# Block 0 of a fused attention and gated feed-forward kernel, laid out with two tokens per row

## Chip, cores, metric

One core of one Trainium2 chip. The metric is the device time in microseconds (us) of one execution. The profile's span of an execution is some 1.8 us shorter than its time; both are used here, and it is said which.

## The reference

Linear attention with a decay per head, then a feed-forward layer with a sigmoid gate. The sizes are B = 4 batches, H = 8 heads, S = 768 tokens, D = 64, d_model = 512 and d_ff = 1536.

```python
def _attn_ref(q, k, v, lam):            # cut: shapes and casts
    for b in range(nb):                 # blocks along the sequence
        intra = einsum('bhic,bhjc->bhij', qb, kb) * Dmask     # lam**(i-j) for i >= j, else 0
        intra = einsum('bhij,bhjd->bhid', intra, vb)
        inter = einsum('bhid,bhde->bhie', qb * lam_pow, kv_state)
        out[block] = intra + inter
        kv_state = lam_block * kv_state + einsum('bhsd,bhse->bhde', kb * rev_pow, vb)

def _moe_ref(x, w_gate, w_val, w_out):
    gate = 1.0 / (1.0 + np.exp(-(x @ w_gate)))
    return gate * (x @ w_val) @ w_out
```

The kernel takes blocks of C = 128 tokens, six in all, which gives the same result. It works in bf16 with sums in 32 bits.

## The kernel before

Block 0 has to be loaded, transposed, scored, masked and multiplied before the first gate product can start; from then on the six blocks are interleaved so that TensorE (PE) always has work. Loads go out from Pool's queue, stores and the transposing copies of later blocks from SP's queue. Cuts are marked.

```python
    osb = ctx.enter_context(tc.tile_pool(name="osb", bufs=4))       # output buffers "ob"
    # ... other pools; PSUM: ps_at 5 banks, ps_ff 3 banks

    def load(n, what, b0, b1):
        # ... (blocks 2 and later: even and odd heads apart)
            nc.gpsimd.dma_start(                # one token per partition, pieces of 64 values
                out=lst[n][:, b0:b1],
                in_=src[b0:b1, :, sl, :].rearrange("b h s d -> s (b h) d"))

    # constants: iotas, identity and triangle on Pool; masks "mask" (DVE) and decay table "lamq" (ACT)
    # are built before the first block is worked on

    def idle(n):                                # filler: keeps PE's clock up while loads are under way
        for i in range(n):
            nc.tensor.matmul(wm, lhsT=zero[:, :128], rhs=zero, start=True, stop=True, ...)

    def c(n, *pairs):                           # state products: 32 for all of block 0
        # ...
                        nc.tensor.matmul(cp[half(u), i, hp, :], lhsT=kdh(n, 2 * bp + i, h),
                                         rhs=V[n][:, 2 * bp + i, h, :], ...)

    def piece_po(n, tt):
        # ... output product of 128 tokens
        ob = osb.tile([128, DM], FP32, tag="ob", name="ob")
        nc.scalar.copy(ob, po)
        nc.sync.dma_start(out=out[tt * S + n * C:tt * S + (n + 1) * C, :], in_=ob)

    load_gv(0, GW)
    idle(10)
    piece_tq0([0, 1])                           # transposes of q, scaled by lamq on DVE
    idle(4)
    piece_tk0(0)                                # transposes of k, copied by ACT
    idle(2)
    piece_s(0, [0])                             # scores
    piece_m(0, 0)                               # masked on DVE (one half of two batches on Pool)
    # ... the other three batches, load_gv(1), load_gv(2), fillers
    piece_a0(0); piece_a0(1); idle(2); piece_a0(2); piece_a0(3, True); idle(2)   # intra products

    make_kd(0)                                  # Pool
    load_gv(3, GW)
    # ... further loads
    gv(0, 0, 1, 2, 3, 4)                        # gate and value products, five of twelve
    c(0, 0, 1)
    # ...
```

Of the kernel before, what the change touches and what calls it, by code (L numbers as in the profile page):

```python
# [16 lines left out]
def kernel(  # L17
# [78 lines left out]

    nc.scalar.preload_act_table_set("natural_log_exp_and_others")
    ident = const.tile([128, 128], BF16, tag="ident")
    zero = const.tile([128, TCH], BF16, tag="zero")
    jn = const.tile([128, 2], FP32, tag="jn")  # L100
    ip1 = const.tile([128, C], FP32, tag="ip1")
    tri = const.tile([128, C], FP32, tag="tri")
    nc.vector.memset(zero, 0.0)  # L103
    nc.vector.memset(ident, 0.0)
    nc.vector.memset(tri, 0.0)
    Sb = stp.tile([128, B, HP, D], BF16, tag="Sb", name="Sb")
    nc.vector.memset(Sb, 0.0)

    load(0, "q", 0, 2)
    load(0, "k", 0, 2)  # L110
    for i, base in enumerate((-1, C - 1)):
        nc.gpsimd.iota(jn[:, i:i + 1], pattern=[[0, 1]], base=base, channel_multiplier=-1,
                       allow_small_or_imprecise_dtypes=True)
    make_identity(nc, ident, nomemset=True)
    nc.gpsimd.iota(ip1, pattern=[[1, C]], base=1, channel_multiplier=0,
                   allow_small_or_imprecise_dtypes=True)
    nc.gpsimd.affine_select(out=tri, in_=tri, compare_op=ALU.is_gt, fill=1.0, base=0,
                            pattern=[[-1, C]], channel_multiplier=1)
    load(0, "k", 2, 4)
    load(0, "q", 2, 3)  # L120
    load(0, "q", 3, 4)
    load(0, "v", 0, 2)
    load(0, "v", 2, 3)
    load(0, "v", 3, 4)

    lnl = const.tile([128, H], FP32, tag="lnl")
    nc.scalar.activation(lnl, lam_bc, AF.Ln)
    pk = const.tile([128, H], FP32, tag="pk")
    nc.scalar.activation(pk, lnl, AF.Exp, scale=jn[:, 0:1])
    lnp = const.tile([128, HP], FP32, tag="lnp")  # L130
    for u in range(2):
        us = slice(u * 64, (u + 1) * 64)
        nc.scalar.activation(lnp[us, :].rearrange("p (e x) -> p e x", e=2),
                             lam_bc[us, :].rearrange("p (x u e) -> p u e x", u=2, e=2)[:, u], AF.Ln)
    lamq = const.tile([128, HP, C], BF16, tag="lamq")
    for hp in range(HP):
        nc.scalar.activation(lamq[:, hp, :], ip1, AF.Exp, scale=lnp[:, hp:hp + 1])
    kds = const.tile([128, H], FP32, tag="kds")
    nc.scalar.activation(kds, lnl, AF.Exp, scale=jn[:, 1:2])
    dec = const.tile([128, HP], FP32, tag="dec")  # L140
    nc.scalar.activation(dec, lnp, AF.Exp, scale=float(C))
    nc.scalar.preload_act_table_set("sigmoid_and_others")
    mask = const.tile([128, 2, HP, C], FP32, tag="mask")
    for u in range(2):
        nc.vector.tensor_tensor(
            out=mask[:, u].rearrange("p (e x) c -> p e x c", e=2),
            in0=tri.unsqueeze(1).unsqueeze(1).to_broadcast([128, 2, 2, C]),
            in1=pk.rearrange("p (x u e) -> p u e x", u=2, e=2)[:, u].unsqueeze(3).to_broadcast([128, 2, 2, C]),
            op=ALU.mult)
# [6 lines left out]

    def transpose(out, x, b, g):
        for u in range(2):
            nc.tensor.transpose(out[half(u)], x[:, b, head(g, u), :], ident)  # L159

    wm = ps_ff.tile([128, TCH], FP32, name="wm", tag="ff")

    def idle(n):
        for i in range(n):
            nc.tensor.matmul(wm, lhsT=zero[:, :128], rhs=zero, start=True, stop=True,  # L165
                             skip_group_check=True)
# [22 lines left out]
    def piece_tq0(bs):  # L189
        tq = ps_at.tile([128, 2, 2, 2 * C], BF16, name="tq", tag="ps")  # L190
        for b in bs:
            if (0, b // 2) not in QS:
                QS[0, b // 2] = trsb.tile([128, 2, 2, 2, C], BF16, tag="QS", name="QS")
            for g in range(HP):
                transpose(tq[:, b % 2, g // 2, g % 2 * C:g % 2 * C + C], Q[0], b, g)
        for b in bs:
            nc.vector.tensor_tensor(out=QS[0, b // 2][:, :, b % 2].rearrange("p e x c -> p e (x c)"),
                                    in0=tq[:, b % 2], in1=lamq_e, op=ALU.mult)

    def piece_tk0(bp):  # L200
        tk = ps_at.tile([128, 2, 2, 2 * C], BF16, name="tk", tag="ps")
        for i in range(2):
            for g in range(HP):
                transpose(tk[:, i, g // 2, g % 2 * C:g % 2 * C + C], K[0], 2 * bp + i, g)
        KS[0, bp] = trsb.tile([128, 2, 2, 2, C], BF16, tag="KS", name="KS")
        for i in range(2):
            nc.scalar.copy(KS[0, bp][:, :, i].rearrange("p e x c -> p e (x c)"), tk[:, i])
# [32 lines left out]
    def piece_m2(n, b, part):  # L240
        if part:
            nc.vector.tensor_tensor(out=MT[n, b][:, 0], in0=SP[n, b][0], in1=mask[:, 0], op=ALU.mult)
            return
        MT[n, b] = mtp.tile([128, 2, HP, C], BF16, tag="MT", name="MT")
        sc = const.tile([128, HP, C], FP32, tag="sc", bufs=2)
        nc.scalar.copy(sc, SP[n, b][1])
        nc.gpsimd.tensor_tensor(out=MT[n, b][:, 1], in0=sc, in1=mask[:, 1], op=ALU.mult)

# [4 lines left out]

    def intra(n, b, out, m, start, stop):
        for e in range(2):
            nc.tensor.matmul(out[half(e)], lhsT=V[n][:, b, 2 * m + e, :],  # L256
                             rhs=MT[n, b][:, m % 2, 2 * e + m // 2, :],
                             start=start, stop=stop, skip_group_check=True)

    def piece_a(n, pairs):  # L260
# [12 lines left out]
        for bp in pairs:  # L273
            for u in range(2):
                for i in range(2):
                    for x in range(2):
                        intra(n, 2 * bp + i, OP[bp, u][:, x, i, :], 2 * x + u, False, i == 1 and x == 1)
# [6 lines left out]
    def piece_a0(b, split=False):  # L284
        if 0 not in XT:
            XT[0] = xtp.tile([128, NMT, B, C], BF16, tag="XT", name="XT")
        w = 2 if split else NMT
        for m0 in range(0, NMT, w):
            op = ps_at.tile([128, w, C], FP32, name="op", tag="ps")
            for m in range(w):  # L290
                intra(0, b, op[:, m, :], m0 + m, m == 0, m == w - 1)
            if split and m0 == 0:
                nc.vector.tensor_copy(XT[0][:, m0:m0 + w, b, :], op)
            else:
                nc.scalar.copy(XT[0][:, m0:m0 + w, b, :], op)
# [28 lines left out]
    def c(n, *pairs):  # L324
        for bp in pairs:
            pool, tag = (ps_at, "ps") if bp == 0 else (ps_ff, "ff")
            cp = pool.tile([128, 2, HP, D], FP32, name="cp", tag=tag)
            for i in range(2):
                for hp in range(HP):
                    for u in range(2):  # L330
                        h = head(hp, u)
                        nc.tensor.matmul(cp[half(u), i, hp, :], lhsT=kdh(n, 2 * bp + i, h),  # L332
                                         rhs=V[n][:, 2 * bp + i, h, :], start=(i == 0 and hp == 0),
                                         stop=(i == 1 and hp == HP - 1), skip_group_check=True)
            dst = Sb[:, 2 * bp:2 * bp + 2]
            if n == 0:
                nc.vector.tensor_copy(dst, cp)
            else:
                nc.vector.tensor_tensor(out=dst, in0=cp, in1=SD.pop(bp), op=ALU.add)  # L339
# [50 lines left out]
    def piece_po(n, tt):  # L390
# [6 lines left out]
        nc.sync.dma_start(out=out[tt * S + n * C:tt * S + (n + 1) * C, :], in_=ob)  # L397
# [5 lines left out]
    idle(10)  # L403
    piece_tq0([0, 1])
    idle(4)
    piece_tk0(0)
    idle(2)
    piece_s(0, [0])
    piece_m(0, 0)
    piece_s(0, [1])  # L410
    piece_m2(0, 1, 0)
    piece_tk0(1)
    piece_tq0([2])
    piece_m2(0, 1, 1)
    load_gv(1, GW)
    idle(3)
    piece_tq0([3])
    piece_s(0, [2], ps_ff, "ff")
    piece_m2(0, 2, 0)
    piece_m2(0, 2, 1)  # L420
    load_gv(2, GW)
    piece_s(0, [3])
    piece_m(0, 3)
    idle(3)
    piece_a0(0)
    piece_a0(1)
    idle(2)
    piece_a0(2)
    piece_a0(3, True)
    idle(2)  # L430

    make_kd(0)
    load_gv(3, GW)
    load(1, "qk", 0, 2)
    load_gv(4, GW)
# [7 lines left out]
    def t(n, bp):  # L443
        piece_t(n, bp)
# [19 lines left out]
    gv(0, 0, 1, 2, 3, 4)  # L464
    c(0, 0, 1)
    fade()
    make_kd(1)
    gv(0, 5, 6, 7)
# [7 lines left out]
    gv(0, 11)  # L476
    t(1, 1)
    load(2, "qkv", 0, B)
    transpose_by_dma(2)
    gvh(1, 0, 0, 1)  # L480
# [89 lines left out]
```

## Time and profile before

| | us |
|---|---|
| time, median of 3 runs | 230.43 (230.3 to 230.69) |
| span of the profiled execution, which was not one of the three and took 231.89 | 230.1 |
| first gate product starts | 19.17 |
| block 0's first output product starts | 67.92 |
| block 3's first gate product starts | 126.75 |

The first view is the chain of waits on the page: the work that ended last, followed back to the start, as shares of the span by engine and then by line.

```profile
PE 92%; DMA 3%; POOL 2%; issue 1%; DVE 0%; POOLq 0%
PE po L393 26%; PE gp L348 25%; PE vp L354 24%; DMA qb<-in_q_dram 3%; PE sp L235 3%; PE gp L365 3%; PE op L256 3%; PE vp L371 3%; PE op L268 1%; PE wm L165 1%; PE cp L332 1%; PE po L382 1%; POOL kb L84 1%; PE tq L159 1%; PE tk L159 0%
```

PE is the limit. Anything that is not PE work is at the start, which the same chain gives piece by piece (start, length, what):

```profile
5.80 6.72 DMA qb<-in_q_dram
...
16.05 0.94 PE wm L165 x3
19.34 0.86 PE gp L348 x4
20.20 0.86 PE vp L354 x4
```

The windows view gives the busy time of each engine in stretches of the span; PEclk is the clock granted to PE, 1.00 being full.

```profile
core 0: us, PE busy (x) PEld busy (x) DVE busy (x) ACT busy (x) POOL busy (x), PEclk, DMA share, GB/s
12.00:16.00 4.00, 3.37 (x45) 1.80 (x41) 1.96 (x4) 1.55 (x3) 2.69 (x3) 0.62 2.04 172
20.00:25.00 5.00, 5.00 (x24) 2.25 (x23) 1.75 (x3) 1.79 (x3) 5.00 (x5) 1.00 0.97 124
25.00:30.00 5.00, 4.95 (x52) 2.46 (x52) 2.89 (x5) 1.59 (x3) 5.00 (x7) 1.00 1.78 157
85.00:100.00 15.00, 14.80 (x155) 7.73 (x156) 4.02 (x6) 6.20 (x11) 9.74 (x8) 1.00 0.50 115
```

From 20 us on PE is busy almost without a gap.

From the view of the output tensor, the time from issue to landing, and from the timeline of SP's queue the first block's stores and the two transposing copies that block 3 needs (start, length):

```profile
DMA to landing us min/median/max: 1.7/2.0/6.1
```

### The profile page before, as it was taken

Reading aid. Unit: us, or ns where it says so; the run is one execution under the profiler, and the core shown is the slowest. Engines: PE = TensorE matmul, PEld = TensorE weight load, DVE = VectorE, ACT = ScalarE, POOL = GpSimd, SP = SyncE. Lnnn points to the kernel's source line nnn. Section 1 sums busy time; section 2 is a strip of 40 time slices with the busy share of each in tenths; the row PEclk is TensorE's granted clock in tenths of the full one; section 3 lists DMA queues with packets and bytes.
Section 4 is the critical chain, followed back from the end, with each engine's and each line's share of the span. In section 5 each row is a group of like instructions: output and inputs, shape, how many; then the busy total and the mean of one; then the engine's idle time right before and its main releaser. Section 6 shows DMA issues by size and latency. Waiting matters only on the chain.

```text
span 230.1 us, 4267 instructions
## 1 busy us (share of the span) xinstructions
PE 220.9 (96%) x1766; PEld 112.1 (49%) x1790; DVE 95.3 (41%) x157; ACT 80.5 (35%) x147; POOL 81.9 (36%) x78
## 2 busy tenths in 40 slices
PE   7689999999999999999999999999999999999994
PEld 2344444688544446444446444446444445444442
DVE  3352456485341352244752244662244750333300
ACT  5525334544332224434224433224433224433221
POOL 8979998693980003970002970000000000000000
PEclk9979999999999999999999999999999999999999
DMA  8999999999999922799912799912740012100022
GB/s 52 144 177 174 122 181 170 182 198 158 152 158 153 218 108 91 159 145 144 57 48 94 153 139 147 68 46 94 151 78 0 3 46 94 46 0 0 3 91 91
DMA packets 102595, 24.92 MB, mean 108 GB/s; under 512 B 91696, under 2 KB 99632, under 8 KB 102576
## 3 DMA queue, kind: packets, MB, share of 16 engines
q0 software_dynamic: 82192, 14.16, 95.2%
q1 hardware_dynamic: 20384, 10.49, 19.1%
q8 instruction: 14, 0.23, 0.4%
q14 instruction: 5, 0.04, 0.1%
HBM read 28.32 MB, written 6.29 MB: 150 GB/s over the span
## 4 chain that ended last, share of the span: by engine, by line
PE 92%; DMA 3%; POOL 2%; issue 1%; DVE 0%; POOLq 0%
PE po L393 26%; PE gp L348 25%; PE vp L354 24%; DMA qb<-in_q_dram 3%; PE sp L235 3%; PE gp L365 3%; PE op L256 3%; PE vp L371 3%; PE op L268 1%; PE wm L165 1%; PE cp L332 1%; PE po L382 1%; POOL kb L84 1%; PE tq L159 1%; PE tk L159 0%
## 5 line engine op out<-in xcount | busy, mean ns | idle before, releaser
L357 DVE TENSOR_TENSOR ht<-sg,vp 128x512 bf16<-128x512 bf16 x65 | 44.7, 688 | 78.6 <-PE vp L354 74.4
L348 PE MATMUL gp<-XT,WG 128*128 128x512 bf16 x252 | 66.2, 379 | 0.7 <-issue 0.2
L354 PE MATMUL vp<-XT,WV 128*128 128x512 bf16 x256 | 65.9, 379 | 0.0
L351 ACT ACTIVATE sg<-gp 128x512 bf16<-128x512 f32 x65 | 38.8, 597 | 70.8 <-PE gp L348 70.6
L393 PE MATMUL po<-WO,ht 128*128 128x512 bf16 x266 | 61.3, 379 | 0.5
L393 PEld LDWEIGHTS <-ht 128*128 128x128 bf16 x276 | 26.2, 98 | 31.2
L354 PEld LDWEIGHTS <-WV 128*128 128x128 bf16 x260 | 25.4, 98 | 30.7
L348 PEld LDWEIGHTS <-WG 128*128 128x128 bf16 x260 | 24.8, 98 | 29.5 <-issue 0.3
L252 DVE TENSOR_TENSOR MT<-sp,mask 128x512 bf16<-128x512 f32 x44 | 27.8, 683 | 14.4 <-PE sp L235 14.4
L396 ACT COPY ob<-po 128x512 f32<-128x512 f32 x23 | 13.5, 585 | 52.5 <-PE po L393 45.8
L317 POOL TENSOR_TENSOR sd<-Sb,dec 128x512 f32<-128x512 bf16 x8 | 8.1, 1035 | 44.9 <-DVE Sb L339 44.8
L308 POOL TENSOR_TENSOR kd<-kb,kds 128x1024 bf16<-128x1024 bf16 x6 | 11.3, 1905 | 4.0 <-DMA kb<-in_k_dram 4.0
L84 POOL DMA_DIRECT2D vb<-in_v_dram x9 | 12.2, 1367 | 0.0
L339 DVE TENSOR_TENSOR Sb<-cp,sd 128x512 bf16<-128x512 f32 x8 | 5.2, 686 | 15.5 <-PE cp L332 15.5
L282 ACT CAST XT<-op 128x512 bf16<-128x512 f32 x20 | 10.4, 598 | 3.0 <-PE op L256 3.0
L165 PE MATMUL wm<-zero 128*128 128x512 bf16 x24 | 9.1, 515 | 1.7 <-DVE zero L103 1.2
L78 POOL DMA_DIRECT2D qb<-in_q_dram x8 | 9.5, 1185 | 0.0
L78 POOL DMA_DIRECT2D kb<-in_k_dram x8 | 9.2, 1171 | 0.0
L365 PE MATMUL gp<-XT,WG 128*128 128x256 bf16 x56 | 8.4, 273 | 0.0
L371 PE MATMUL vp<-XT,WV 128*128 128x256 bf16 x56 | 8.4, 272 | 0.0
L302 POOL TENSOR_TENSOR kd<-kb,kds 128x1024 bf16<-128x1024 bf16 x4 | 7.6, 1912 | 2.1 <-DMA kb<-in_k_dram 2.1
L375 DVE TENSOR_TENSOR ht<-sg,vp 128x256 bf16<-128x256 bf16 x14 | 5.8, 419 | 5.1 <-PE vp L371 4.1
(59 smaller groups left out, 124.9 us busy)
## 6 DMA issues: line engine op xcount, KB each, us to landing
out_dram<-ob SPq DMA_DIRECT2D x23, 256.0 KB, 2.0
kb<-in_k_dram POOLq DMA_DIRECT2D x12, 256.0 KB, 9.9
qb<-in_q_dram POOLq DMA_DIRECT2D x11, 256.0 KB, 8.7
vb<-in_v_dram POOLq DMA_DIRECT2D x4, 512.0 KB, 13.3
WG<-in_moe_w_gate_dram POOLq DMA_DIRECT2D x6, 256.0 KB, 7.3
WV<-in_moe_w_val_dram POOLq DMA_DIRECT2D x6, 256.0 KB, 7.9
WO<-in_moe_w_out_dram POOLq DMA_DIRECT2D x3, 512.0 KB, 14.2
vb<-in_v_dram POOLq DMA_DIRECT2D x3, 256.0 KB, 10.5
```

The source lines that it names most:

```text
L78: nc.gpsimd.dma_start(out=lst[n][:, e].rearrange("p b y d -> p (b y) d"), in_=src[:, e::2, sl, :].rearrange("b y s d -> s (b y) d"))
L84: nc.gpsimd.dma_start(out=lst[n][:, b0:b1], in_=src[b0:b1, :, sl, :].rearrange("b h s d -> s (b h) d"))
L165: nc.tensor.matmul(wm, lhsT=zero[:, :128], rhs=zero, start=True, stop=True, skip_group_check=True)
L252: nc.vector.tensor_tensor(out=MT[n, b][:, u], in0=SP[n, b][u], in1=mask[:, u], op=ALU.mult)
L348: nc.tensor.matmul(gp, lhsT=WG[:, mt, fs], rhs=x[:, mt, :], start=(mt == 0), stop=(mt == NMT - 1))
L351: nc.scalar.activation(sg, gp, AF.Sigmoid)
L354: nc.tensor.matmul(vp, lhsT=WV[:, mt, fs], rhs=x[:, mt, :], start=(mt == 0), stop=(mt == NMT - 1))
L357: nc.vector.tensor_mul(HT[n, ft], sg, vp)
L365: nc.tensor.matmul(gp[:, cs], lhsT=WG[:, mt, fs], rhs=x[:, mt, cs], start=(mt == 0), stop=(mt == NMT - 1))
L371: nc.tensor.matmul(vp[:, cs], lhsT=WV[:, mt, fs], rhs=x[:, mt, cs], start=(mt == 0), stop=(mt == NMT - 1))
L393: nc.tensor.matmul(po, lhsT=HT[n, ft][:, tt * 128:(tt + 1) * 128], rhs=WO[:, ft, :], start=(ft == 0), stop=(ft == NFT - 1))
L396: nc.scalar.copy(ob, po)
```

## The change

The intent is to start the gate products sooner. Block 0's q, k and v are laid out with two neighbouring tokens in one row: a batch's 128 tokens take 64 partitions, two batches share a tile, and a piece of the load is 128 values long instead of 64. So there are half as many pieces, and one load per batch. The products of block 0 then run on quarters of the PE array (64 x 64), and its tokens come out in a permuted order (even tokens, then odd ones), which the store has to undo. Pool loses its iotas (DVE makes the constants), and the second weight slice is issued before Pool's one mask product. The tables that only blocks 1 and later need are made on DVE between the first gate products.

```diff
+    R = 2
+    SR = C // R
+    Q0, K0, V0 = (qkv.tile([128, NB2, H, R, D], BF16, tag=c + "b", name=c + "b") for c in "qkv")
+    def load0(t, src, b):
+        nc.gpsimd.dma_start(
+            out=t[b % 2 * 64:b % 2 * 64 + 64, b // 2].rearrange("p h r d -> p h (r d)"),
+            in_=src[b, :, 0:C, :].rearrange("h (s r) d -> s h (r d)", r=R))
+    # ... twelve loads: q0 k0 q1 k1 q2 q3 k2 k3 v0 v1 v2 v3; constants on DVE in place of Pool's iotas
+    def make_lamq():
+        nc.vector.tensor_copy(lamq.rearrange("p g (s r) -> p g r s", r=R),
+                              lam0.rearrange("p g (r s) -> p g r s", r=R))
+        nc.vector.tensor_scalar(out=tri, in0=ip1, scalar1=p1, scalar2=None, op0=ALU.is_ge)
+    def make_mask(u):
+        nc.vector.tensor_tensor(out=mask[:, u]..., in0=tri..., in1=pk..., op=ALU.mult)
+    # ... turn0, piece_s0, piece_a0: transposes, scores and intra products on 64 x 64 quarters
+    def piece_c0():                       # 64 state products instead of 32
         ob = osb.tile([128, DM], FP32, tag="ob", name="ob")
         nc.scalar.copy(ob, po)
-        nc.sync.dma_start(out=out[tt * S + n * C:tt * S + (n + 1) * C, :], in_=ob)
+        dst = out[tt * S + n * C:tt * S + (n + 1) * C, :]
+        nc.sync.dma_start(out=dst.rearrange("(s r) m -> r s m", r=R) if n == 0 else dst, in_=ob)
     GW = DFF // 6
     load_gv(0, GW)
-    idle(10)
-    piece_tq0([0, 1])
-    idle(4)
-    piece_tk0(0)
-    # ...
+    idle(6, True)
+    piece_tq0(0)
+    idle(1)
+    piece_tk0(0)
+    # ... scores of the second pair of batches:
+    piece_s0(1)
+    load_gv(1, GW)
+    piece_m0(1, 0, 0, True)               # Pool's mask product
+    # ... intra products of both pairs, fillers
     load_gv(2, GW)
     load_gv(3, GW)
     load(1, "qk", 0, 2)
+    make_kd0()                            # Pool's state product
-    gv(0, 0, 1, 2, 3, 4)
-    c(0, 0, 1)
+    gv(0, 0)
+    make_lamq()
+    gv(0, 1)
+    make_mask(0)
+    gv(0, 2)
+    make_mask(1)
+    gv(0, 3, 4, 5, 6)
+    piece_c0()
     # ... t(1, 1) half a gate product later
```

## The prediction

> **What bounds it now.** The chain of waits is 92% PE; from 19.2 us on PE is back to back (windows view: 9.95 of 10 us busy from 20 to 30, 14.79 of 15 from 30 to 45). All that can be won is the start: the first gate product begins at 19.17 us (timeline). Before it the chain reads: Pool issuing loads to 5.80, a q load landing at 12.5, then transposes, scores, masks, intra products and filler matmuls. Issue-to-landing times give landings of q01 6.3, k01 8.4, k23 11.5, q2 12.5, q3 13.4, v3 16.4, WG0 17.7, WV0 19.05, WG1 20.4, WV1 21.8. The granted clock is 0.59 and 0.72 from 12.5 to 17.5 us (windows).
>
> **What changes.**
> - Two tokens per row halve the descriptors of block 0. From q01 to v3, 1280 KB (as written) landed in 10.1 us, 127 KB/us; v3 to WV1, with pieces four times as long, 1024 KB in 5.4 us, 190 KB/us. A line through the two gives about 163 KB/us for the new pieces (estimate), so block 0's 1.5 MB takes 9.4 instead of 12 us. This fits the Trainium skill, "DMA: Bandwidth & Descriptors", section Specifications, which wants at least 512 B per piece for line rate. Pool spacing per issue is 1.14 us (2048 pieces), 0.86 (1024), 0.74 (512-piece weights); I take 0.74 for the twelve new loads. The iotas leave Pool (0.9 us).
> - Estimated landings: q0 4.7, k1 7.0 to 8.5, k3 10.1 to 11.7, v3 13.3 to 14.9, WG0 14.7, WV0 16.
> - Then the chain is on ACT and DVE: lam0 ready about 6.1, KS copies, seven small ACT tables (about 1.4 us) before the second KS copy, about 8.5; first pair's scores; four mask products (0.68 each) and two scalings (0.42) on DVE to about 12.4; second pair's masks to about 14.5; intra products, copies (0.42 each). Ideal gate start 15.7; such sums come out about 0.8 us early, so 16.6 us.
> - Pool's product (1.3 us) waits for the second weight slice's issues (ending about 13.1), about when its input is ready: little cost. In return slice 2 lands before it is needed (19.5 us).
> - Cost: block 0's state products become 64 quarter-array matmuls instead of 32. Before, 32 took 0.63 us; the existing 64x64 products take 22 ns each, so about 1.4 us: +0.8 us on PE's path. The Trainium skill, "TensorEngine Tiling (Array Packing)", section Instruction Overhead, warns not to take tiling from a dimension already small; 64 columns is that case. The extra mask tables fall on DVE, which has room (0.69 of each 1.73 us used).
>
> **Sum.** Gate start 19.2 to 16.6 saves 2.6; state products give back 0.8; 0.3 for slips: about 1.5 us. Everything after block 1 is unchanged PE work. Predicted 228.9 us, range 227.4 to 230.4. Chances: faster by over 2% 0.04, within 2% 0.93, slower by over 2% 0.03.
>
> **What would show it.** First gate matmul between 15.6 and 17.6 us; last block 0 k landing near 11 instead of 11.5-13.4; Pool issues of block 0 at about 0.74 us each; state products 1.2 to 1.6 us; the rest of the chain still PE, same stretches of the same length, no new DMA wait at the gate products.
>
> **What would make it wrong.** Loads into 64 partitions using fewer engines, so landing no sooner; self-dependent small DVE operations delaying ident and masks; the table load holding back the KS copies; a colder clock at the gate start (filler cut from ten to six at first) costing up to 1 us; weight slices becoming the limit (WV0 cannot be used before about 16 us), which caps the gain near 3 us; DVE products plus four state copies holding PSUM buffers and stalling PE.

## More of the kernel before

```profile
71.32 22.02 SPq L397 DMA_DIRECT2D out_dram<-ob  x8
93.45 2.00 SPq L176 DMA_TRANSPOSE QR<-qb  x1
95.55 2.89 SPq L176 DMA_TRANSPOSE KR<-kb  x1
```

The two copies are issued at 93 and 95 us, long before block 3's scores.

## The result

| | before | after |
|---|---|---|
| time, median of 4 runs, us | 230.37 (230.3 to 230.69) | 239.02 (238.37 to 239.62) |
| span of the profiled execution | 230.1 | 237.1 |
| first gate product starts | 19.17 | 18.58 |
| block 0's first output product starts | 67.92 | 69.66 |
| block 3's first gate product starts | 126.75 | 133.31 |

The ratio is 1.037, with a 95% interval of 1.034 to 1.040: slower. A ratio here is the mean time of one kernel's fast runs over the mean of the other's in the same rounds, so it is not quite the ratio of the medians. All runs counted were fast.

Differences of the rows give a budget of the 7.0 us between the two spans: -0.6 before the first gate product; +2.3 from there to the first output product (48.75 before, 51.08 after); +4.8 from there to block 3's gate products (58.83 before, 63.65 after); +0.4 for the rest. So there are two losses, both in stretches that the prediction took as unchanged, and hardly any gain at the start.

The medians differ by 8.65 us and the spans by 7.0, because the profiled execution of the kernel before, at 231.89 us, was slower than any of its timed runs, and slow at the start. Against the usual execution that b_look shows below (230.15 us, span 228.4, with the same marks at 17.13, 66.19 and 125.02) the budget is 8.7 us: +1.5 before the first gate product, then +2.0, +4.8 and +0.4. By that look the start is a third loss.

### Second stretch: 20 to 30 us

The windows view of the changed kernel:

```profile
core 0: us, PE busy (x) PEld busy (x) DVE busy (x) ACT busy (x) POOL busy (x), PEclk, DMA share, GB/s
20.00:25.00 5.00, 3.92 (x19) 1.67 (x17) 4.42 (x4) 1.44 (x3) 5.00 (x5) 1.00 1.28 160
25.00:30.00 5.00, 4.17 (x19) 1.85 (x19) 4.14 (x6) 1.19 (x2) 5.00 (x6) 1.00 2.10 166
85.00:100.00 15.00, 12.04 (x141) 6.13 (x140) 3.02 (x6) 4.21 (x8) 8.00 (x6) 1.00 0.28 99
```

PE has lost 1.9 us between 20 and 30 us, and DVE is now busy 8.6 of 10 us. The timeline of the same stretch (start, length, engine, line, what; in brackets the idle time before it and what ended it):

```profile
21.18 1.75 DVE L200 COPY lamq<-lam 128x512 bf16<-128x512 bf16 x1
...
21.41 1.19 POOL L84 DMA_DIRECT2D kb<-in_k_dram  x1
...
22.57 3.95 POOL L393 TENSOR_TENSOR kd<-kb,kd 128x1024 bf16<-128x1024 bf16 x2
...
22.83 1.92 DVE L202 TENSOR_SCALAR tri<-ip,tok 128x128 f32<-128x128 f32 x1
...
25.26 1.81 DVE L205 TENSOR_TENSOR mask<-tri,pk 128x512 f32<-128x512 f32 x1
25.39 1.02 PE L458 MATMUL gp<-XT,WG 128*128 128x512 bf16 x4 [1.47 <-DVE ht L467]
...
27.59 0.68 DVE L205 TENSOR_TENSOR mask<-tri,pk 128x512 f32<-128x512 f32 x1
27.72 1.02 PE L458 MATMUL gp<-XT,WG 128*128 128x512 bf16 x4 [0.44 <-DVE ht L467]
```

The two masks are the same operation on the same shapes. The first, begun while Pool's state product (kd) is running, takes 1.81 us; the second, begun after it, takes 0.68. The small triangle, 128 values per partition, takes 1.92 us. While DVE is held up, the product ht of gate and value waits behind it, keeps its two PSUM banks, and PE stops: 1.47 and 0.44 us.

### Third stretch: 80 to 118 us

The chain of waits, shares of the span and then pieces in order of time:

```profile
PE 75%; DMA 14%; SPq 3%; DVE 3%; issue 1%; ACT 1%; POOL 1%; ACTq 0%; DVEq 0%; POOLq 0%
```

```profile
69.82 10.38 PE po L503 x48
80.22 0.59 ACT ob L506
80.83 17.49 DMA out_dram<-ob
98.43 0.59 ACT ob L506
99.59 6.59 SPq L240
106.28 11.48 DMA KR<-kb
117.81 0.62 PE sp L351 x16
```

An output store has taken a place in the chain. ACT waits for stores to land before it can reuse an output buffer, and what PE needs from ACT comes late (two stops of PE, 1.5 and 1.3 us, by the view of its waits); SP, which issues stores and transposing copies in one order, comes to block 3's copies at 99.59 instead of 93.45; the copies take longer to issue and to land; and block 3's scores wait for them (1.3 us). The view of ACT's waits (us in total, times, longest) has a line that the kernel before doesn't have:

```profile
ACT ob L506 <- DMA out_dram<-ob: 11.2, 3, 4.5
```

The view of the output tensor has a new maximum, and SP's queue is later and slower:

```profile
DMA to landing us min/median/max: 1.7/2.2/14.8
```

```profile
73.06 26.31 SPq L508 DMA_DIRECT2D out_dram<-ob  x8
99.59 6.59 SPq L240 DMA_TRANSPOSE QR<-qb  x1
106.28 5.76 SPq L240 DMA_TRANSPOSE KR<-kb  x1
```

The 14.8 us are those of block 1's first store, which SP issues behind block 0's four; for the four themselves the trace has no landing.

The edit says what is different about block 0's four stores. Before, a store writes 128 rows of 512 values, 128x512. After, block 0's write 2x64x512: the permutation has put a dimension of size 2 outermost. (In the trace's operands, `dst_num_elem=[128,1]` has become `[64,2]` for these four.) The packets in the trace show what that does. A store has 128 packets of 2 KB; the table gives the stretch from the first packet's start to the last one's end, and how many were under way at a time (the sum of their lengths over the stretch):

```
                                stretch us    under way    one packet, ns
before, a store in steady state      0.82         13            85
after, block 0, first store          5.45          2.1          89
after, block 0, second store         5.13          2.1          84
```

A packet takes as long as ever; there are two at a time instead of thirteen.

### The start

The new loads behaved much as predicted. Landings, from issue and time to landing: the last k at 11.65 us (estimated 10.1 to 11.7), the last v at 14.55 (13.3 to 14.9). Pool took 0.68 to 0.82 us for each of the new issues (0.74). But the first weight slices landed at 16.62 and 18.00 us, not at 14.7 and 16, and the gate began at 18.58, not 16.6. In the usual execution of the kernel before (b_look) the last v landed at 15.58 us and the slices at 16.73 and 18.07. So the new layout brought block 0's last v 1.0 us sooner, and the weights that the gate and value products also need only 0.1 us.

### The profile page after: what moved, and what is told of

The parts are those of the page before. It is cut to its first block, busy times and chain, and to the rows that moved or that the text cites. A ratio compares the mean times of both kernels' runs of the same rounds, so it can differ in the third digit from the quotient of the medians.

```text
span 237.1 us, 4639 instructions
## 1 busy us (share of the span) xinstructions
PE 223.9 (94%) x1946; PEld 113.4 (48%) x1946; DVE 105.6 (45%) x191; ACT 80.8 (34%) x152; POOL 80.0 (34%) x76
## 3 DMA queue, kind: packets, MB, share of 16 engines
q0 software_dynamic: 76112, 14.16, 82.0%
q1 hardware_dynamic: 20328, 10.49, 20.2%
## 4 chain that ended last, share of the span: by engine, by line
PE 75%; DMA 14%; SPq 3%; DVE 3%; issue 1%; ACT 1%; POOL 1%; ACTq 0%; DVEq 0%; POOLq 0%
PE po L503 21%; PE gp L458 19%; PE vp L464 19%; DMA out_dram<-ob 7%; DMA KR<-kb 5%; SPq L240 3%; PE gp L475 3%; PE vp L481 2%; DMA kb<-in_k_dram 2%; PE sp L351 2%; PE wm L229 2%; PE op L379 2%; PE po L492 1%; PE op L369 1%; PE tp L262 1%
## 5 line engine op out<-in xcount | busy, mean ns | idle before, releaser
L458 PE MATMUL gp<-XT,WG 128*128 128x512 bf16 x260 | 66.9, 379 | 4.9 <-DVE ht L467 1.9
L464 PE MATMUL vp<-XT,WV 128*128 128x512 bf16 x260 | 66.7, 379 | 0.0
L503 PEld LDWEIGHTS <-ht 128*128 128x128 bf16 x276 | 26.3, 98 | 31.2
L359 DVE TENSOR_TENSOR MT<-sp,mask 128x512 bf16<-128x512 f32 x40 | 25.2, 682 | 13.3 <-PE sp L351 13.3
L421 POOL TENSOR_TENSOR kd<-kb,kds 128x1024 bf16<-128x1024 bf16 x6 | 11.4, 1906 | 0.7 <-DMA kb<-in_k_dram 0.6
L84 POOL DMA_DIRECT2D vb<-in_v_dram x6 | 9.3, 1543 | 0.0
L478 ACT ACTIVATE sg<-gp 128x256 bf16<-128x256 f32 x14 | 5.4, 384 | 7.0 <-PE gp L475 7.0
## 6 DMA issues: line engine op xcount, KB each, us to landing
vb<-in_v_dram POOLq DMA_DIRECT2D x4, 512.0 KB, 14.2
WO<-in_moe_w_out_dram POOLq DMA_DIRECT2D x3, 512.0 KB, 13.3
```

Source lines behind the costliest of these rows:

```text
L359: nc.vector.tensor_tensor(out=MT[n, b][:, u], in0=SP[n, b][u], in1=mask[:, u], op=ALU.mult)
L421: nc.gpsimd.tensor_tensor(out=KD[n][:, e], in0=K[n][:, e], in1=kds[:, e::2].unsqueeze(1).unsqueeze(3).to_broadcast([128, B, HP, D]), op=AL ...
L458: nc.tensor.matmul(gp, lhsT=WG[:, mt, fs], rhs=x[:, mt, :], start=(mt == 0), stop=(mt == NMT - 1))
L464: nc.tensor.matmul(vp, lhsT=WV[:, mt, fs], rhs=x[:, mt, :], start=(mt == 0), stop=(mt == NMT - 1))
L503: nc.tensor.matmul(po, lhsT=HT[n, ft][:, tt * 128:(tt + 1) * 128], rhs=WO[:, ft, :], start=(ft == 0), stop=(ft == NFT - 1))
```

## The experiments

Theory S: the store's outermost dimension of 2 keeps it on few DMA engines; this is the third stretch's loss. Its rival is the row order itself: every second row of the output, an address pattern and not a shape. Theory P: DVE's tables wait for Pool; this is the second stretch's loss. Its rival D: DVE's new tables are slow, or too many, by themselves. Theory C: PE ran at half clock through much of the changed start. Its rival: the weight slices' landing sets the gate's start.

The kernel before was run again beside each set: 230.89 us (median of 7) beside the first four runs, 230.05 (one run) beside the three looks, 230.77 (11 runs) beside the two warmer kernels and the one with less filler, and 230.98 and 230.84 (7 each) beside the last two.

### a_store: block 0's store as two stores of 64 rows

The change, with the same rows going to the same addresses by other shapes:

```diff
-        nc.sync.dma_start(out=dst.rearrange("(s r) m -> r s m", r=R) if n == 0 else dst, in_=ob)
+        if n == 0:
+            for r in range(R):
+                nc.sync.dma_start(out=dst.rearrange("(s r) m -> r s m", r=R)[r],
+                                  in_=ob[r * SR:(r + 1) * SR])
+        else:
+            nc.sync.dma_start(out=dst, in_=ob)
```

> The changed kernel with block 0's store made as two stores of 64 rows each, one for each token of the pair; rows still go to every other row of the output. Theory S (a store whose outermost dimension is 2 is spread over few DMA engines, lands in 10 to 15 us and holds the output buffers, ScalarE and so TensorE): stores of block 0 land in 2 to 6 us as in the kernel before, no wait of ScalarE for an output store, about 4.8 us come back: 234.2 us. Rival (alternate rows in memory, or the loads of block 3 beside them, are what is slow): stores stay slow, 238 to 239 us.

Measured: 233.67 us (232.98 to 234.44), ratio to before 1.012 (1.008 to 1.015), correct. ACT no longer waits for a store; block 3's copies are issued at 94.98 and 97.35 us and take 2.27 and 2.82. The rows still go to every second row of the output, so the address pattern is not the cause; the shape is. This is 5.4 us of the loss (239.02 less 233.67; the two medians are from different sets of runs).

### a_tables: the tables four gate products later

```diff
-    gv(0, 0)
+    gv(0, 0, 1, 2, 3, 4)
     make_lamq()
-    gv(0, 1)
+    gv(0, 5)
     make_mask(0)
-    gv(0, 2)
+    gv(0, 6)
     make_mask(1)
-    gv(0, 3, 4, 5, 6)
```

> The changed kernel with the late tables (lamq copy, tri, two masks) on VectorE after gate products 4, 5 and 6 instead of 0, 1 and 2, so after Pool's state product of block 0 (which ended at 26.5 us). Theory P (VectorE operations with their inputs in SBUF wait while Pool's product runs): tri back from 1.92 to about 0.2 us, first mask from 1.81 to 0.68, no TensorE gap at the second and third gate products, about 2.1 us come back: 236.9 us. Rival (the tables are simply too much or too slow work for VectorE between the gate products): the same gap, later; 238.5 to 239.5 us.

Measured: 240.34 us (238.29 to 241.66), ratio 1.040 (1.033 to 1.046). The time was missed, the mechanism not: the tables now take 0.45, 0.99 and 0.68 us, no gate product waits for DVE, and from the first gate product to the first output product it takes 48.85 us, as in the kernel before. But in the profiled run the gate started at 20.84 us, so that the output products began at 69.69, where they began in the changed kernel (69.66); and the rest, with block 0's first store now spread over 7.0 us, was 2.4 us longer. The gain of this part could not be seen as time while the stores were there and the start wandered. It had to be measured with the stores mended.

### a_both: both edits

The two edits above together.

> Both repairs. If the two losses are separate and additive: 239.0 - 4.8 - 2.1 = 232.1 us. If they overlap (the delay at the tables hides part of the store delay): 233 to 235 us. If the start of the changed kernel is really worth 1.5 us as predicted: 229 us.

Measured: 232.06 us (231.88 to 233.08), ratio 1.006 (1.003 to 1.010), correct. Against a_store it is 1.6 us less, which is what the tables' place cost in time once the stores were mended (the ranges of the two just touch). The stretch from the first gate product to the first output product is 48.85 us (48.75 before). What is left, 1.2 us, lies ahead of the gate, which began at 19.50 us in this profile.

### b_store: the kernel before, with the new form of store alone

The result is wrong: rows that are not permuted are stored as if they were.

```diff
-        nc.sync.dma_start(out=out[tt * S + n * C:tt * S + (n + 1) * C, :], in_=ob)
+        dst = out[tt * S + n * C:tt * S + (n + 1) * C, :]
+        nc.sync.dma_start(out=dst.rearrange("(s r) m -> r s m", r=2) if n == 0 else dst, in_=ob)
```

> The kernel before with only the new store form of block 0 (alternate rows, outermost dimension 2); its rows come out in the wrong order on purpose. Theory S: stores land in 10 to 15 us, ScalarE waits for output stores, time 230.4 + 4.8 = 235.2 us. Rival (something else in the changed kernel slows that stage): 230 to 231 us.

Measured: 241.53 us (239.01 to 243.02; one of the four runs was slow), ratio of the fast ones 1.042 (1.035 to 1.049). The direction is that of theory S, the size twice what was expected. ACT's wait for stores, in its view of waits:

```profile
ACT ob L396 <- DMA out_dram<-ob: 20.2, 4, 6.1
```

The first two stores spread over 7.0 and 6.7 us, not 5.3, with 1.8 packets under way. Block 3's loads were under way beside them: the load of v for block 3, issued at 66.5 us, landed 31.2 us later (in the kernel before after 14.3 to 14.4). It is likely that the two slow each other on the engines that they share; the trace doesn't say which engine moves a packet. The longest stop of PE, 5.4 us, was for a copy of block 2's intra result that ACT could make only after standing 6.1 us in front of a store. So what such a store costs depends on what happens to be loading beside it; why this kernel fared worse than the changed one beyond that was not taken apart.

### b_law: four outermost sizes, where nothing else loads

The kernel before with block 4's four stores reshaped, to outermost sizes of 16, 8, 4 and 2. Its output is wrong, which doesn't matter for the time.

```diff
+        if n == 4:
+            dst = dst.rearrange("(s r) m -> r s m", r=16 >> tt)
```

> The kernel before, with the four stores of block 4 (a quiet stage for loads) written with outermost dimensions of 16, 8, 4 and 2 in this order (rows in wrong order on purpose). Theory S: time to landing grows as the outermost dimension shrinks, about 2, 2.5 to 3, 4 and 6 us or more; with 16 no slower than the plain form (2.0). Rival (alternate rows are what is slow): all four alike, 16 being the most scattered and no better than 2.

One look, 230.21 us beside 230.05. From the packets:

```
outermost size    stretch us    under way
128 (others)           0.82         13
16                     1.27         12.3
8                      2.44          7.1
4                      4.33          3.7
2                      6.26          2.1     (overlaps the one before it)
```

The number of packets under way follows the outermost size, up to 16, and each halving makes the stretch 1.4 to 1.9 times as long. The size of 16 was not quite as quick as the plain form (1.27 us against 0.82, landing after 2.93 us against 2.0, where no loss was expected); for the three smaller sizes the trace has no landing, so the stretches have to serve. This is what the Trainium skill says, in "DMA: Bandwidth & Descriptors", section "Why a DMA increments its semaphore by 16 and not by 1": the number of engines is the largest one up to 16 that divides the slowest dimension that isn't of size 1, on both sides of the transfer. The same page's "Rules for kernel authors" has it as a rule: "Put a dim whose size is a multiple of 16 (ideally the 128 partitions) outermost". The time did not move, and ACT's view of waits has no wait for a store: the cost of such a store is not its length but what queues behind it.

### a_nokd: the changed kernel without Pool's state product

Wrong: the state is computed from k without its decay.

```diff
-    make_kd0()
+    KD[0] = K0
```

> The changed kernel without Pool's state product of block 0 (the keys are used unscaled: wrong result on purpose), the tables left where they are. Theory P: tri takes about 0.2 us and both masks 0.68, no TensorE gap at gate products 2 and 3; about 2 us faster than the changed kernel, near 237 us. The lamq copy tells a side question: if it drops well below 1.75 us it too was waiting on Pool, if not it is slow in itself. Rival (tables too slow in themselves): durations as in the changed kernel, 239 us.

One look. The time, 240.38 us, was not the 237 expected; as in a_tables the gate began later (19.38 us) and the stretch of the stores took longer. But no gate product waits for DVE, and from the first gate product to the first output product it takes 48.84 us, as in the kernel before. DVE's timeline, with the tables at their place between the first gate products:

```profile
21.98 0.45 DVE L200 COPY lamq<-lam 128x512 bf16<-128x512 bf16 x1
22.32 0.89 DVE L202 TENSOR_SCALAR tri<-ip,tok 128x128 f32<-128x128 f32 x1
...
23.70 0.69 DVE L205 TENSOR_TENSOR mask<-tri,pk 128x512 f32<-128x512 f32 x1
```

At the same place and without Pool's product the triangle takes 0.89 us instead of 1.92 (not 0.2 as expected) and the first mask 0.69 instead of 1.81: theory P, and not D. The Trainium skill, "SBUF — State Buffer", section "Who interferes with whom", states it: a DVE instruction with two SBUF inputs contends with a Pool instruction that reads SBUF, copies and operations with a scalar may contend in a two-port mode, and whoever comes first holds the shared ports for its whole instruction. The mask has two SBUF inputs, the copy and the triangle one. The copy lamq (1.75 us in the changed kernel) began before Pool's product, beside Pool's issuing of loads, and was done 0.36 us after the product began. Here it took 0.45 us, and here too Pool was issuing a load beside it (of k, 21.87 to 23.18 us); in a_both it took 0.47 us beside an issue. So issuing alone did not hold it up there, and what did in the changed kernel stays open.

### b_look: the kernel before, once more

> The kernel before, unchanged, for a second look at its start. The first profile had a granted clock of 0.59 to 0.72 from 12.5 to 17.5 us. If that is peculiar to that execution, the first gate product comes about 1 to 1.5 us before 19.17 us here, and the changed start (18.58 us) gained nothing; if it belongs to the kernel, 19.2 us again.

One look, 230.15 us beside 230.05 for the kernel before. The line of the timeline to read is the first gate product:

```profile
17.13 1.02 PE L348 MATMUL gp<-XT,WG 128*128 128x512 bf16 x4
```

It starts at 17.13 us and not at 19.17, at full clock. In two further profiles of the kernel before with a change only later on, b_law and b_store, it starts at 17.53 and 17.87. The first profile, on which the prediction stands, was the late one.

### a_warm: both edits, and more filler

First fillers eight instead of six, six instead of two behind the first key transposes, one more at three places further on, one less at one.

```diff
-    idle(6, True)
+    idle(8, True)
     ...
-    idle(2)
+    idle(6)
     ...
+    idle(1)
     piece_tk0(1)
     ...
-    idle(2)
+    idle(3)
     piece_s0(0)
     ...
```

> Both repairs, and more filler matmuls on TensorE in the start (8 instead of 6 first, 6, 1 and 3 instead of 2, 0 and 2 in the waits for loads, one more before the last key transposes, one fewer before the last intra products). Theory C (the changed start loses because TensorE runs at half clock from about 6 to 13 us, its filler having been cut): fillers and transposes at full rate after about 8 us, first gate product near 17.2 us instead of 18.1 to 20.8, then bound by WV0's landing (18.0); time 230.0 to 230.9, against 232.1 for both repairs alone. Rival (the start is bound by the loads and the VectorE chain whatever the clock): first gate product at 18.5 us or later, 231.5 to 232.5 us.

Measured: 230.21 us (229.68 to 233.85, where one of six runs was slow), ratio 0.9965 (0.994 to 0.999), correct. That is 1.9 us less than a_both, from filler alone. The reason can be read from the fillers themselves in the timelines. The changed kernel, and then a_both:

```profile
9.31 1.04 PE L229 MATMUL wm<-zero 128*128 128x512 bf16 x2
...
14.19 0.60 PE L229 MATMUL wm<-zero 128*128 128x512 bf16 x2
```

```profile
14.37 0.61 PE L229 MATMUL wm<-zero 128*128 128x512 bf16 x1
```

In the changed kernel the same two fillers take 1.04 us at 9.3 us and 0.60 at 14.2: PE ran at about half rate until some 12 us. In a_both's profile, where the start is the same program, a single filler still takes 0.61 us at 14.4. In a_warm:

```profile
8.38 0.82 PE L229 MATMUL wm<-zero 128*128 128x512 bf16 x3
...
13.69 0.28 PE L318 MATMUL op<-MT,vb 64*64 64x128 bf16 x6
15.69 0.58 PE L318 MATMUL op<-MT,vb 64*64 64x128 bf16 x26 [1.73 <-issue]
```

Three fillers in 0.82 us: full rate already. The gate nevertheless began only at 18.02, not at 17.2 as expected, because of the last line: PE stood still for 1.73 us in the middle of 32 intra products and waited for no semaphore ("issue").

### a_split: the first weight slice in two halves

```diff
     GW = DFF // 6
-    load_gv(0, GW)
+    for lo in range(0, GW, 128):
+        nc.gpsimd.dma_start(out=WG[:, :, lo:lo + 128], in_=wg_r[:, :, lo:lo + 128])
+        nc.gpsimd.dma_start(out=WV[:, :, lo:lo + 128], in_=wv_r[:, :, lo:lo + 128])
```

> As a_warm, with the first weight slice loaded in two halves of 128 columns, so that the first gate and value products need half the bytes. If WV0's landing is the limit at the warm clock: first value product about 1 us sooner after the block's loads, 0.3 to 0.8 us faster than a_warm, 229.3 to 230.4 us. Rival (the limit is elsewhere, or the smaller pieces cost more than they free): same as a_warm or slower by up to 0.5 us.

Measured: 230.08 us (229.65 to 231.42, six runs), ratio 0.998 (0.995 to 1.000); gate at 17.75 us, the same stop of 1.57 us. As good as a_warm and no better: the first slices landed at 15.75 and 16.54 us, but with the stop there their landing was not what PE waited for. So a run that settles the rival to theory C, the slices' landing, is missing.

### b_idle6: the kernel before, with less filler

```diff
-    idle(10)
+    idle(6)
```

> The kernel before with its first filler matmuls cut from ten to six, as the change did, and nothing else. Theory C: the clock is not or less often released in the start, fillers of 0.43 us each after 6 us, first gate product 1 to 2 us later than its usual 17.1 to 17.9; 231 to 232.5 us. Rival: no difference, 230.2 to 230.9 us.

Measured: 230.67 us (230.36 to 231.2, six runs), ratio 0.999 (0.997 to 1.001): no difference. PE was at half rate until about 9 us in it, but at full rate by 9.6, and at 18.61 us its value products waited for the weights to land. For the kernel before, theory C missed: a cold start of that length is hidden behind the loads. That it cost the changed kernel time because there it lasted into the scores and the second pair's work is a reading of the two timelines and was not tested.

### a_fetch: what is the stop in a_warm?

The stop sits at the 448th PE instruction (weight loads and products counted) in a_warm and a_split, and also, with 0.39 and 0.18 us, in the changed kernel and a_store, although there other products stand at that place. So a number in the program, not an operand, seems to decide it. To shift the number, a_warm's first eight fillers of 512 columns become four each of 128 columns, 48 instructions more.

```diff
-    idle(8, True)
+    idle(8, True, True)          # each filler as four of 128 columns
```

> a_warm with its first eight filler matmuls of 512 columns each replaced by four of 128 columns: the same PE work, 48 more PE instructions ahead of everything else. In a_warm PE stood still for 1.73 us inside block 0's intra products at its 448th instruction, waiting for no semaphore; in three other kernels the stop fell on the same number at other operations. Theory I (PE's instructions for what follows have not arrived yet, their fetch queues behind the loads): the stop moves 48 instructions earlier in the program, into the second pair's score products, which break in two about 13.3 us and go on only at 15 to 15.7; the intra products then run with no such stop of their own. Rival W (the intra products wait for data, the last v load or a mask product): the score products run unbroken in about 0.85 us from 13.1, and the stop of 1.5 us or more stays inside the intra products. Time about 230 to 231 us under either.

Measured: 229.48 us (229.24 to 231.25, five runs), ratio 0.994 (0.991 to 0.998), correct. For its question it was inconclusive. The profiled run was the slowest of the five; PE was at half rate until 9.6 us in it, reached the second scores at 14.87 us only, and the timeline shows no stop. Both theories allow that, if what was missing had arrived by then. (From start to start, though, there is a trace of one: the 15th of the second scores, which is the 448th instruction here, begins 0.21 us after the 14th, at 15.44 us; in the changed kernel that step is 0.04 us.)

### a_fetch2: the same question with PE kept warm

a_warm, with one of its six fillers behind the first key transposes replaced by twelve of 64 columns: 22 instructions more.

```diff
-    idle(6)
+    idle(5)
+    for i in range(12):
+        nc.tensor.matmul(wm[0][:, :64], lhsT=zero[:, :128], rhs=zero[:, :64], start=True, stop=True, ...)
```

> The run before left PE at half clock until 9.6 us, so it reached the place in question only at 15 us and could not tell. This one keeps a_warm's first fillers whole and puts 12 filler matmuls of 64 columns in place of one of 512 columns behind the first key transposes: 22 PE instructions more, some 0.3 us of work. Theory I (PE's instructions have not arrived): the stop still falls at PE's 448th instruction, which is now the 28th of the 32 score products of the second pair; those start about 13.3 us, break off after 27, and go on about 15.5. Rival W (the intra products wait for data): the scores run unbroken in about 0.85 us and the stop of 1.5 us or more comes after 6 or 7 intra products, as in a_warm, or after another number of them. If PE is again late (second scores not before 14.5 us) the run tells nothing. Time about 230 to 231 us under either.

Measured: 229.57 us (229.44 to 231.15, four runs), ratio 0.996 (0.992 to 1.000), correct. The timeline of PE:

```profile
13.18 0.79 PE L290 MATMUL sp<-QS,KS 64*64 64x128 bf16 x27
14.64 0.27 PE L290 MATMUL sp<-QS,KS 64*64 64x128 bf16 x5 [0.68 <-issue]
14.72 0.63 PE L318 MATMUL op<-MT,vb 64*64 64x128 bf16 x32
...
17.19 1.02 PE L458 MATMUL gp<-XT,WG 128*128 128x512 bf16 x4
```

The scores break off after exactly 27 of 32, which is the 448th instruction again, and the intra products run unbroken. So the stop belongs to a place in the instruction stream and not to data: theory I's place, shown. It was shorter here, 0.68 us, and the gate began at 17.19 us, the earliest start seen in a changed kernel. The traces also have an "instruction" queue whose packets are 16 KB each. In all five profiles with the stop PE went on 1.33 to 1.54 us after the end of the first such packet of the execution (in a_fetch2 it moved from 12.15 to 13.10 us; in a_warm to 14.16, and PE went on at 15.69). In a_both, a_tables and a_nokd, which have no stop, PE came to that place only 2.1 to 3.1 us after the packet's end. The small step in a_fetch ends 1.48 us after it. So it is very likely that PE waited for its instructions. That their supply is held up by the loads is less sure; no run varied the loads to show it. The Trainium skill, "Runtime: NRT & Kernel Launch", section "Instruction fetch mechanics", says that each engine fetches its instructions by DMA in blocks of 16 KB and that the cost of crossing one is "mostly hidden"; here, at the start, up to 1.7 us of it was not, if this is what it was.

## Why the prediction was wrong

The prediction was 228.9 us, range 227.4 to 230.4, with a chance of 0.03 for slower by over 2%. Measured were 239.02 us. Point by point:

- **What bounds the kernel: right.** PE, 92% of the chain.
- **"Everything after block 1 is unchanged PE work": the step that failed, by 5.4 us.** The PE work is unchanged, but block 0's store is not, and the prediction doesn't name it at all: not among what the change moves, nor among what would make it wrong. Its shape, 2x64x512, leaves two packets under way at a time instead of thirteen; four such stores hold ACT (11.2 us of waits), SP's queue, and through it block 3's copies and scores. Shown by a_store (-5.4 us, same rows and addresses in another shape), b_store (the form alone makes the kernel before 4.2% slower) and b_law (the law). It could have been costed beforehand: 128 packets of 85 ns, two at a time, are an estimated 5.4 us a store, where the trace of the kernel before shows 0.82.
- **"The extra mask tables fall on DVE, which has room": failed, by 1.6 us in time** (a_store to a_both), 2.3 us in the stretch. The busy share of DVE was read rightly, but it is not room: Pool's state product ran from 22.57 to 26.52 us, and DVE's tables wait for it, shown by a_nokd. A mask costed at 0.68 us took 1.81.
- **Gate start, 16.6 us for 19.2: failed in both numbers.** The 19.17 us of the first profile were an outlier: 17.13 to 17.87 in the later looks at the kernel before. Even with 16.6 the gain would have been 0.5 to 1.3 us, not 2.6. And the changed kernel's gate began at 18.58. (The 0.8 us that the prediction adds to its ideal sum rests on no run of this case.) Of the reasons that the prediction listed as risks, the colder clock was real: more filler took 1.9 us off (a_warm), more than the "up to 1 us" that it allowed. The first weight slices landed 2 us later than estimated and so no sooner than in the kernel before (18.00 us for the second, against 18.07 in b_look): the faster loads did not reach what the gate waits for. Why the slices fell behind the line through two rates was not tested; a_split shows no gain from halving the slice, but had the stop. In profiles of changed kernels the gate began at 17.19 us at the earliest. A stop at the 448th PE instruction, 0.4 us in the changed kernel and up to 1.7 in the others, was in no list.
- **Block 0's landings: right**, inside the ranges for the last k and the last v.
- **State products +0.8 us: the term was mis-sized.** 64 quarter-array products took 0.67 us, where 32 took 0.63: +0.04. The estimate of 22 ns each came from existing 64 x 64 products with 128 columns; these have 64 columns and come to about 10 ns each (0.67 / 64). The Trainium skill, "TensorEngine Tiling (Array Packing)", section Instruction Overhead, was cited for a warning that did not apply here: by the page the overhead is that of some 60 columns, and these products have 64.
- **Pool's mask product behind the weight issues costs little: right.** Among the changed kernels only a_fetch's profile shows PE waiting for it, 0.6 us.

The sum from the runs, in medians: 239.02, less 5.35 for the stores, less 1.61 for the tables, less 1.85 for a warmer PE, is 230.21. By the ratios, which compare within a set of runs, the three are about 5.9, 1.3 and 2.2 us. The order matters, too: the tables moved alone made the time no better (a_tables, 1.040 against 1.037), and after that the mended stores were worth 8.3 us (240.34 less 232.06), so the two losses partly hide each other. With all three the changed kernel is 0.35% faster than before (a_warm), and the variants with some fillers split stand at ratios of 0.994 and 0.996. That is not the earlier gate that was meant: in these four profiles it begins at 17.19 to 18.73 us, in the usual ones of the kernel before at 17.13 to 17.87. Where the gain comes from was not taken apart. The intervals overlap, so none of the variants is shown to be the best, but a_warm and a_fetch beat both the kernel before and the changed one.

Two things stay open besides: what held up the copy lamq in the changed kernel, and whether the loads delay the instructions that PE waits for at the 448th. The warmth of PE also varies from run to run of the same kernel (a_fetch's profiled run was cold, and it was its slowest), which a single profile doesn't show.

## What to carry to other kernels

When a change permutes data, follow it to the store, and look at the outermost dimension of every transfer: a size of 2 there made a store six times as long, and what queued behind it cost 5 us that no engine's busy share foretold. Idle time on DVE is only room if Pool isn't computing at the time; put DVE's tables where it doesn't (beside Pool's issuing of loads the two masks took 0.68 us each in a_tables). And look twice at the kernel before: one profile gave a start that was 2 us late, and the whole expected gain was read from it.

## What the Trainium skill lacked or had wrong

- "DMA: Bandwidth & Descriptors" had the rule, and it held: with an outermost size of 16, 8, 4 and 2 there were 12.3, 7.1, 3.7 and 2.1 packets under way. It lacks what such a store does to others: a load under way beside such stores landed 31.2 us after its issue instead of about 14, and ACT waited 20.2 us in all (b_store).
- "SBUF — State Buffer" held (first mask 1.81 us beside Pool's product, 0.69 without it). It lacks an example of what follows: DVE held up keeps PSUM banks, and PE stopped for 1.47 us.
- "TensorEngine Tiling (Array Packing)" was not wrong here, but applied wrongly. It lacks a measured time for products on 64 x 64 quarters: here 64 products of 64 columns took 0.67 us together, about 10 ns each.
- "TensorE: Matmul & The Clock Gate", section "Seeing it yourself", warns that clock records can be unreliable. The windows view of the changed kernel gave 1.00 from 8 to 12 us, where two fillers took 1.04 us instead of 0.60. Durations of fillers were the better measure.
- "Runtime: NRT & Kernel Launch" calls the cost of crossing an instruction block mostly hidden. PE stood still for 1.73 us (a_warm) and 0.68 us (a_fetch2) at the same instruction number, waiting for no semaphore; if that was an instruction fetch, it was not hidden. No page has such a stop at the start of a kernel.
